# The way back of an FFT convolution: 32-row TensorE tiles, 32x32 transposes on VectorE, and another token order

## The chip, the cores and the metric

The kernel runs on one core of a Trainium2 chip. The metric is the device time of one execution in microseconds (us). The kernel before was run three times; its time is the median of the three. A profile comes from one further execution. Engines are named as in the profile: PE is TensorE's matrix products and PEld its weight loads, DVE is VectorE, ACT is ScalarE, POOL is GpSimd, SP is SyncE, whose queue issues nearly all transfers.

## The reference

One layer of a model: a gated long convolution and an MLP, each behind a layernorm whose scale and shift come from a conditioning vector. There are 2048 tokens and 640 channels, everything in float32.

```python
mod = (silu(c) @ w_mod)                  # six rows of 640: sa, ca, ga, sb, cb, gb
h = layernorm(x) * (1 + ca) + sa         # x is A_q, 2048 x 640
# k_shift: causal convolution of k with 4 taps a channel
kv = k_shift * v
# causal convolution over all 2048 tokens, channel by channel, by FFT of length 4096
y = irfft(rfft(kv, 4096) * rfft(ssm_k, 4096))[:2048] + kv * ssm_D
x = x + ga * (h * y)
h = layernorm(x) * (1 + cb) + sb
out = x + gb * (relu(h @ w1 + b1) ** 2 @ w2 + b2)
```

## The kernel before

**Transform part.** Channels go in five blocks of 128 (index b). The FFT of length 4096 is written as matrix products in two steps each way, with tables `cw` and `gb` on the way there and `gi` and `ca` on the way back. For a block the kernel does this:

- `kv_load`, `kv_k`, `kv_s`, `kv_v`, `kv_m` (four pieces of 512 tokens): load k and v, transpose them with TensorE into PSUM, apply the four taps on VectorE (`kv_s` reads the transposed k, `kt`, from PSUM), multiply by v, and store to the scratch `kv_d`. `load_x` brings that back with time split over the partitions; `load_h` does so for the filter.
- `unit_a` (first step there): 32 products with 64x64 tiles of the array, evicted by ACT into `AX`.
- `front(b, j)`, j = 0 to 7: `spectrum` of the filter (`h`) and of the data (`x`) with `gb`, in two halves of 64 columns; the complex product by VectorE and POOL into `wr` and `wi`.
- `back(b, j)`, j = 0 to 3, one for two fronts: first step back. 16 products with a 64x128 stationary piece of `gi`, in two row halves of 64, into two PSUM tiles `qp` of 512 columns, which two ACT copies scatter into `QT`.
- `unit_t(b, g)`, g = 0 to 7: four 128x128 transposes of `QT` by TensorE into PSUM, then one ACT copy of 512 columns to SBUF.
- `unit_y(b, g)`: second step back. 16 products of 64 moving columns with `ca` as the moving operand; after each second one, 512 columns of y go to the block's tile `UPt`, by ACT for b < 3, by VectorE for b = 3, and for b = 4 as the product with the normalised x that already stands there (the last one in two parts, the second in `y_rest`).
- `prep_a`, `prep_m`, `prep_p`: ACT normalises x into `UT` (for the last block into `UPt`), VectorE scales, POOL shifts. `gate` multiplies by y on VectorE; `finish_near` and `finish_add` add the residual and store to the scratch `x1_d`.

In between stand the products and sums of the conditioning rows (`part_load`, `part_scale`, `part_add`, `mod_row`, `mod_col`) and the statistics of x (`stats1`).

**Order.** Every engine runs its instructions in the order of the program (`keep_order`). For block b there are 10 front slots, FS(b, 0..9), each with a `front` while j < 8 and a `back` at j = 3, 5, 7 and 9; then 18 second-stage slots, GS(b, 0..17) (11 for the last block). The table `tab` puts the rest into slots by hand; the calls of a slot come after its `back` or units, or before them if the slot is in the set `AFTER`. `UNITS` gives for each block the second-stage slots of `unit_a` (of block b + 1), `unit_t` and `unit_y`. Tags name buffers: PSUM has four buffers X, two Y and two T; S4 holds `QT`, S5 `gb`, S6 `gi`, UP0 and UP1 the tiles `UPt`. A tile that reuses a buffer waits until the last reader of the old one is done. Two lines of `tab` that matter:

```python
at(FS(0, 1), (kv_k, 1, 0, "T"), (kv_v, 1, 0), (p_tile, 2))
at(FS(0, 3), (kv_s, 1, 0))
```

and so again at FS(0, 5) and FS(0, 7) for the next piece, and at FS(1, 1) and FS(1, 3) for block 2. `mod_row` and `mod_col` use T as well.

**MLP part.** The hidden layer is computed in 82 steps (`mlp_front`), its squares go to the scratch `h_d` with sums and differences of pairs (a Strassen scheme), and the second product runs over eight blocks of 256 tokens (n) and seven pieces (k): `products`, from k = 0 to 5 the Strassen products into eight accumulators of 320 columns, and for k = 6 the plain products of the last hidden rows into four of them. `evict_first` combines accumulators 0 to 3 into the residual `X2` after k = 5, `evict_rest` adds 4 to 7 at the end of the block. For the last block the order of k is 0, 1, 6, 2, 3, 4, 5, so there both come at the end.

Of the kernel before, what the change touches and what calls it, by code (L numbers as in the profile page):

```python
# [18 lines left out]
P = 128  # L19
# [5 lines left out]
CH = 256  # L25
# [9 lines left out]
def _constants():  # L35
# [16 lines left out]
    gi = np.zeros((2, 64, 2, 64))  # L52
# [10 lines left out]
    gi[0, 1:32, 0], gi[1, 1:32, 0] = 2 * np.cos(ph).T, -2 * np.sin(ph).T  # L63
    gi[0, 0, 0] = 1.0
    gi[1, 0, 0] = (-1.0) ** n1
# [3 lines left out]
    gi[0, 32:, 1], gi[1, 32:, 1] = 2 * np.cos(ph).T, -2 * np.sin(ph).T  # L69

    ca = np.zeros((32, 2, 2, 2, 2, 2, 16, 2))
    t2 = np.arange(16)
    for h in range(2):
        nn = 2 * t2 + h
        th = 2 * np.pi * ((m[:, None] * nn[None, :]) % 64) / 64
        a, b = 2 * np.cos(th) / N, -2 * np.sin(th) / N
        a[0] = 1.0 / N
        b[0] = (-1.0) ** nn / N
        for g in range(2):
            for d in range(2):  # L80
                ca[:, g, d, 0, h, g, :, d] = a
                ca[:, g, d, 1, h, g, :, d] = b
    f = np.float32
    gb = gb.reshape(128, 16, 2, 2, 64).transpose(0, 1, 3, 2, 4)
    gt = gb.transpose(3, 4, 1, 2, 0).copy()
    gt[0, :, 0] = gi.reshape(2, 64, 128).transpose(1, 0, 2)
    return {
        "cw": cw.astype(f),
        "ca": ca.reshape(128, 256).astype(f),
        "gb": gb.reshape(128, 4096).astype(f),  # L90
        "gi": gt.reshape(128, 4096).astype(f),
# [4 lines left out]
def ssm_mlp_kernel(  # L96
# [72 lines left out]
    TS = [WX[i][:, 4 * j : 4 * j + 4] for i in (2, 3) for j in range(2)]  # L169
# [7 lines left out]
    ca = WX[1][:, 8:10].rearrange("p r (h n) -> p r h n", h=2)  # L177
# [186 lines left out]
    gi = sb.tile([P, 16, 2, P], F32, tag="S6", name="gi")  # L364

    def load_gi(i):
        src = gi_d.rearrange("p (g r n) -> p g r n", g=16, r=2)
        sp_dma(gi[:, 4 * i : 4 * i + 4], src[:, 4 * i : 4 * i + 4])
# [89 lines left out]
    def back(b, j):  # L458
        if j == 0:
            QT[b] = sb.tile([P, DG, 32, 4], F32, tag="S4", name=f"q_{b}")  # L460
        end = b == NB - 1 and j == 3
        t = [
            ps.tile(
                [P, 4, P], F32, tag="X" if end else "Y", name=f"qp_{b}_{j}_{a}", bufs=4 if end else 2
            )
            for a in range(2)
        ]
# [1050 lines left out]
```

## Time and profile before

| | |
|---|---|
| runs, us | 677.71, 680.04, 681.62 (median 680.04) |
| profiled execution | 676.89 us, span 675.0 us |
| granted TensorE clock | 0.995 of full speed (mean) |
| transform part | from the start to about 290 us |
| MLP part | from there to the end; last product ends near 668 us |
| transfers | 130.8 MB, 194 GB/s over the span |

The windows are stretches of the span with the busy time of each engine. A row of the chain of waits is start, length, engine, tile and line, and the number of instructions. A row of the groups has line, engine, operation, tiles and shapes, the count, and then busy time and mean length in ns. A row of the timeline is start, length, engine, line, operation, tiles, and in brackets the idle time before it with what ended it. The lengths of PE instructions in the groups include their way through the array, on which the next ones overlap; what a piece takes is better read from the chain.

### The profile page before, as it was taken

How to read it: one execution, taken by the hardware profiler on the slowest of the kernel's cores; microseconds unless marked ns; L12 is line 12 of the kernel's file. 1: busy time of each engine (PE TensorE's matmuls, PEld its weight loads, DVE VectorE, ACT ScalarE, POOL GpSimd, SP SyncE). 2: the span in 40 equal slices, each digit the busy share in tenths (PEclk: the TensorE clock that was granted, in tenths of full speed). 3: DMA queues.
4: the chain of work that ended last, by engine and by line, in shares of the span. 5: the costliest groups of instructions: out<-in, count | busy, mean ns of one | idle time of the engine just before them, and what ended most of it. 6: DMA issues, size and time to landing. Idle time of an engine off the chain costs nothing.

```text
span 675.0 us, 20357 instructions
## 1 busy us (share of the span) xinstructions
PE 635.5 (94%) x8585; PEld 589.0 (87%) x8585; DVE 396.4 (59%) x682; ACT 377.1 (56%) x741; POOL 317.7 (47%) x377
## 2 busy tenths in 40 slices
PE   6788889999989999999999999999989999999995
PEld 5687878789879898889999898898879999999995
DVE  4266566676757689577873175246846445544462
ACT  4535555877875986567785474376763323333230
POOL 1063146459967978846555179328602202221122
PEclk9999899999999999999999999999999999999999
DMA  9698699869555355456644745355375675456641
GB/s 245 202 280 282 161 248 280 239 202 265 151 167 155 110 139 176 118 203 206 223 189 190 248 149 207 145 190 185 104 272 175 230 241 174 154 208 227 219 150 41
DMA packets 108494, 130.80 MB, mean 194 GB/s; under 512 B 21106, under 2 KB 77298, under 8 KB 108404
## 3 DMA queue, kind: packets, MB, share of 16 engines
q1 hardware_dynamic: 106736, 129.30, 61.4%
q8 instruction: 67, 1.10, 0.7%
q10 hardware_dynamic: 1604, 0.21, 0.2%
q14 instruction: 23, 0.19, 0.1%
q0 software_dynamic: 64, 0.01, 0.0%
HBM read 87.03 MB, written 42.47 MB: 192 GB/s over the span
## 4 chain that ended last, share of the span: by engine, by line
PE 80%; ACT 6%; DVE 5%; DMA 4%; issue 3%; POOL 1%; DVEq 0%; POOLq 0%; SPq 0%; ACTq 0%
PE h L811 24%; PE acc L932 21%; PE y L569 6%; PE pa L392 6%; PE qp L473 5%; PE x L407 4%; PE acc L945 3%; PE h L407 3%; PE t L558 2%; PE kt L248 1%; PE xtp L761 1%; PE vt L285 1%; DMA h_d<-wy 1%; DVE wy L154 1%; DMA KV<-in_A_v_dram 1%
## 5 line engine op out<-in xcount | busy, mean ns | idle before, releaser
L160 POOL TENSOR_TENSOR wy<-wy 128x128 f32<-128x128 f32 (+1 forms) x92 | 59.6, 653 | 87.8 <-DVE wy L160 43.1
L157 POOL TENSOR_TENSOR e<-e,e 128x320 f32<-128x320 f32 x16 | 17.5, 1093 | 142.0 <-ACT e L149 142.0
L811 PE MATMUL h<-xt_S,w_S 128*128 128x256 f32 (+2 forms) x425 | 82.4, 308 | 0.0
L860 ACT ACTIVATE wy<-h,b1e 128x256 f32<-128x256 f32 (+1 forms) x77 | 41.9, 544 | 45.3 <-PE h L811 37.0
L392 PE MATMUL pa<-wx,p 64*64 64x64 f32 x2560 | 51.4, 228 | 14.5 <-issue 9.4
L811 PEld LDWEIGHTS h<-xt_S,w_S 128*128 128x128 f32 x425 | 61.8, 189 | 3.7
L392 PEld LDWEIGHTS pa<-wx,p 64*64 64x64 f32 x2560 | 44.9, 140 | 21.7 <-issue 16.8
L149 ACT ACTIVATE a<-pa 128x512 f32<-128x512 f32 x80 | 43.6, 605 | 28.8 <-PE pa L392 28.5
L154 DVE TENSOR_TENSOR wy<-x,wx 128x512 f32<-128x512 f32 x64 | 41.0, 682 | 18.3 <-ACT wx L149 8.5
L811 PE MATMUL h<-xt_XP,w_S 128*128 128x512 f32 (+1 forms) x160 | 50.4, 358 | 0.0
L157 DVE TENSOR_TENSOR wy<-wy 128x128 f32<-128x128 f32 (+1 forms) x36 | 17.9, 498 | 53.5 <-ACT wy L861 41.6
L569 PE MATMUL y<-wy 128*64 128x64 f32 x1280 | 44.9, 226 | 3.7 <-issue 1.9
L569 PEld LDWEIGHTS y<-wy 128*64 128x64 f32 x1280 | 40.5, 139 | 8.2 <-issue 3.8
L149 ACT ACTIVATE h_S<-c_UP 128x896 fp32r<-128x896 f32 (+2 forms) x32 | 25.7, 816 | 39.1 <-PE acc L932 30.6
L407 PE MATMUL x<-a,gb 128*64 128x128 f32 x640 | 41.8, 274 | 3.1 <-DVE wy L154 1.9
L160 DVE TENSOR_TENSOR h_S<-c_UP,h_S 128x896 fp32r<-128x896 f32 (+2 forms) x32 | 30.7, 970 | 23.9 <-ACT h_S L149 23.7
L861 ACT ACTIVATE wy<-wy 128x256 f32<-128x256 f32 (+1 forms) x82 | 40.7, 497 | 2.6
L270 DVE SCALAR_TENSOR_TENSOR KV<-kt,tap,KV 128x511 f32<-128x511 f32 (+2 forms) x48 | 35.9, 747 | 8.0 <-ACT ktail L149 6.3
L407 PEld LDWEIGHTS x<-a,gb 128*64 128x64 f32 x640 | 35.9, 137 | 4.6 <-PE h L407 2.5
L149 ACT ACTIVATE q<-qp 128x512 f32<-128x512 f32 (+1 forms) x40 | 21.2, 583 | 31.8 <-PE qp L473 31.8
L157 POOL TENSOR_TENSOR wm<-wm,wm 128x640 f32<-128x640 f32 x20 | 32.6, 1632 | 8.7 <-ACT wm L350 8.4
L160 POOL TENSOR_TENSOR we<-wy 128x256 f32<-128x256 f32 x20 | 15.8, 791 | 42.4 <-DVE wy L154 42.3
(215 smaller groups left out, 1636.9 us busy)
## 6 DMA issues: line engine op xcount, KB each, us to landing
c_UP<-h_d SPq DMA_DIRECT2D x48, 448.0 KB, 5.4
h_d<-wy SPq DMA_DIRECT2D x24, 448.0 KB, 2.6
h_d<-wy SPq DMA_DIRECT2D x12, 896.0 KB, 4.5
wm<-in_w_mod_dram SPq DMA_DIRECT2D x25, 320.0 KB, 4.6
KV<-in_A_k_dram SPq DMA_DIRECT2D x20, 256.0 KB, 5.1
KV<-in_A_v_dram SPq DMA_DIRECT2D x20, 256.0 KB, 5.2
xp<-in_A_q_dram SPq DMA_DIRECT2D x5, 1024.0 KB, 6.6
x_d<-x SPq DMA_DIRECT2D x8, 640.0 KB, 3.1
```

What stands on the lines that cost most here:

```text
L149: act.activation(o, i, AF.Copy)
L154: eng.tensor_mul(o, a, b)
L157: eng.tensor_add(o, a, b)
L160: eng.tensor_sub(o, a, b)
L270: dve.scalar_tensor_tensor(o, tk[:, : 512 - t], tap[:, b, t : t + 1], o, op0=ALU.mult, op1=ALU.add)
L392: pe.matmul(t[e][64 * r : 64 * r + 64, g].rearrange("p m d -> p (m d)"), pt[b][l, i, 8 * q + g, :], cw[l, r], start=True, stop=True,)
L407: pe.matmul(t[64 * a : 64 * a + 64, s + r], gb[:, g, r, a], AX[b][i][:, 2 * g + a], start=True, stop=True,)
L569: pe.matmul(y[64 * h : 64 * h + 64, 4 * (g % 2) + i].rearrange("p c l d -> p (c l d)"), tss[g][:, i, 64 * r : 64 * r + 64], ca[:, r, h], s ...
L811: pe.matmul(hps[t, f, c0], w, y, start=(b == 0 and i == 0), stop=(b == NB - 1 and i == len(terms) - 1),)
L860: act.activation(z, h.rearrange("p (n s) -> p n s", n=n), AF.Relu, bias=bias)
L861: act.activation(z, z, AF.Square)
L932: pe.matmul(acc[j], h[a][:, c], w[:, y], start=(first and i == 0), stop=(k == NP - 1 and i == 2 and (j < 4 or last)),)
```

## The change

- **Frequency sets.** The outputs of the second step there (`gb`) are ordered so that a tile of 128 rows holds four sets of 32 frequencies, one for each 32-row strip.
- **`back`.** The new `gi` has half the size. Per `back` there are 32 products, each of 32 rows, 64 stationary and 128 moving columns, over four row strips and two column halves, into four PSUM tiles of 256 columns, with the tags Y, Y, T, T. Four copies evict them into `QT`, now channel by 32 frequencies (by ACT; in the last `back` two of them by VectorE).
- **`unit_t`.** Four a block instead of eight. Each is one VectorE instruction that transposes 32x32 blocks of a 128x1024 piece of `QT` into one of two buffers `TT`, in the room that `gi` gave up. TensorE's transposes and their ACT copies are gone.
- **`unit_y`.** Four a block instead of eight: two products each, with `ca` (now 64 columns) stationary and 512 columns moving, into one PSUM tile, one for each column half. The evictions keep their engine, count and size, in another order of elements.
- **Token order.** In SBUF partition and row are now (w, n) and l for token 32n + 16w + l, where they were l·128 + partition. Loads of q and stores of the result go in two transfers of 64 partitions each (`fetch`, `put`).
- **Slots.** `UNITS` has new slots for `unit_t` and `unit_y`; the u tile is asked for at the first `unit_y` instead of the second. `tab` and `AFTER` are as before.
- **The end.** The last token block takes k in the order 0 to 6, `evict_first` does its sums in another order, and the last stores go over SP and ACT by turns, in eight transfers.

```diff
@@ constants: gb's columns reordered; new gi [4, 32, 16, 2, 2, 32] and ca [128, 64] @@
+        c, s = [t.reshape(64, 32, 2).transpose(0, 2, 1).reshape(64, 64) for t in (c, s)]
...
+    s6 = sb.tile([P, 4096], F32, tag="S6", name="gi")
+    gi = s6[:, 0:2048].rearrange("p (g r n) -> p g r n", g=16, r=2)
+    TT = [s6[:, 2048 + 1024 * i : 3072 + 1024 * i].rearrange("p (c n) -> p c n", n=32) for i in range(2)]
...
     def back(b, j):
         if j == 0:
-            QT[b] = sb.tile([P, DG, 32, 4], F32, tag="S4", name=f"q_{b}")
+            QT[b] = sb.tile([P, P, 32], F32, tag="S4", name=f"q_{b}")
         end = b == NB - 1 and j == 3
         t = [
-            ps.tile([P, 4, P], F32, tag="X" if end else "Y", name=f"qp_{b}_{j}_{a}", ...)
-            for a in range(2)
+            ps.tile([P, 2, P], F32, tag="YYTT"[q], name=f"qp_{b}_{j}_{q}", bufs=2)
+            for q in range(4)
         ]
-        for u in range(4):
-            w = ws[b, 2 * j + u // 2]
+        for i in range(2):
+            w = ws[b, 2 * j + i]
             for r in range(2):
-                for a in range(2):
-                    l = slice(64 * a, 64 * a + 64)
-                    pe.matmul(t[a][:, u], gi[l, 4 * j + u, r], w[r][l, u % 2], ...)
+                for q in range(8):
+                    u, q = (q + q // 4) % 2, q % 4
+                    l = slice(32 * q, 32 * q + 32)
+                    pe.matmul(t[q][64 * u : 64 * u + 64, i], gi[l, 4 * j + 2 * i + u, r], w[r][l, u], ...)
...
+        for q in range(4):
+            m = 8 * j + q
+            copy(dve if q % 2 and end else act, QT[b][:, :, m : m + 5 : 4], t[q].rearrange("p i c -> p c i"))
...
+    def tokens(t, l0, n, cols=slice(0, D)):
+        t = t.rearrange("(n w l) d -> w n l d", w=2, l=NL)
+        return [t[w, :, l0 : l0 + n, cols] for w in range(2)]
+
+    def fetch(t, src):
+        for w in range(2):
+            sp_dma(t[64 * w : 64 * w + 64], src[w])
...
-    def unit_t(b, g):
-        t = ps.tile([P, 4, P], F32, tag="T", ...)          # "X" for the last block
-        for i in range(4):
-            pe.transpose(t[:, i], QT[b][:, 4 * g + i].rearrange("p m d -> p (m d)"), ident)
-        copy(act, tss[g], t)
+    def unit_t(b, k):
+        dve.transpose(TT[k % 2], QT[b][:, 32 * k : 32 * k + 32])
+
+    def unit_y(b, k):
+        y = ps.tile([P, 32, NL], F32, tag="Y", name=f"y_{b}_{k}", bufs=2)
+        for w in range(2):
+            pe.matmul(
+                y[64 * w : 64 * w + 64].rearrange("p c l -> p (c l)"),
+                ca,
+                TT[k % 2][:, :, NL * w : NL * w + NL],
+                start=True, stop=True,
+            )
+        x = 16 * (k % 2)
+        uo = UPt[b].rearrange("p l (x e d) -> p x e d l", e=2, d=2)[:, x : x + 16, k // 2]
+        y = y.rearrange("p (x d) l -> p x d l", d=2)
         if b < NB - 1:
+            copy(act if b < 3 else dve, uo, y)
+        elif k < 3:
+            dve.tensor_mul(uo, y, uo)
...
-    seq = [(n, k) for n in range(NC - 1) for k in range(NP + 1)]
-    seq += [(NC - 1, k) for k in (0, 1, NP, *range(2, NP))]
+    seq = [(n, k) for n in range(NC) for k in range(NP + 1)]
...
     UNITS = [
-        ([0, 2, 4, 11, 11, 16, 16], [1, 3, 3, 5, 5, 6, 7, 9], [3, 4, 4, 6, 6, 8, 9, 10]),
-        ([1, 1, 5, 7, 9, 10, 12], [1, 3, 4, 6, 8, 11, 14, 14], [4, 6, 7, 10, 13, 14, 16, 17]),
-        ([1, 3, 5, 7, 8, 11, 14], [1, 3, 5, 7, 9, 11, 12, 15], [4, 6, 8, 9, 12, 14, 16, 17]),
-        ([0, 3, 4, 6, 9, 11, 14], [1, 3, 4, 7, 9, 11, 13, 14], [4, 6, 8, 10, 13, 14, 16, 17]),
-        ([], [1, 1, 2, 2, 5, 5, 6, 7], [4, 4, 5, 6, 6, 8, 8, 10]),
+        ([0, 2, 4, 11, 11, 16, 16], [1, 3, 5, 7], [3, 5, 7, 9]),
+        ([1, 1, 5, 7, 9, 10, 12], [1, 3, 6, 11], [4, 7, 10, 14]),
+        ([1, 3, 5, 7, 8, 11, 14], [1, 5, 9, 12], [4, 8, 12, 16]),
+        ([0, 3, 4, 6, 9, 11, 14], [1, 4, 9, 13], [4, 8, 13, 16]),
+        ([], [0, 1, 2, 4], [1, 2, 4, 6]),
     ]
...
-            if s == sy[1] and not last:
+            if s == sy[0] and not last:
                 u_tile(b)
```

More of the change, by code (lines that the diff above doesn't have):

```diff
@@ L916, in ssm_mlp_kernel, with products @@
     accs = {}
-    def products(n, k, first, last):
-        if first:
+    def products(n, k):
+        if k == 0:
             acc = accs[n] = []
@@ L971, in evict_rest @@
         last = n == NC - 1
-        for j in (3, 0, 1, 2) if last else range(4):
+        for j in range(4):
             s, c = j // 2, (C0, C1)[j % 2]
```

141 lines of the change are left out of this document (56 added, 85 removed).

## The prediction

> **What bounds the kernel now.** First the page's busy times, then the windows of busy time cut at the transform's stages.
>
> ```profile
> span 675.0 us, 20357 instructions
> PE 635.5 (94%) x8585; PEld 589.0 (87%) x8585; DVE 396.4 (59%) x682; ACT 377.1 (56%) x741; POOL 317.7 (47%) x377
> ```
> ```profile
> 39.00:60.00 21.00, 20.56 (x421) 18.71 (x417) 13.53 (x22) 9.30 (x19) 12.91 (x25) 1.00 0.92 272
> 60.00:90.00 30.00, 23.81 (x677) 21.50 (x679) 18.88 (x40) 15.41 (x30) 3.66 (x12) 0.94 0.73 206
> 90.00:117.00 27.00, 26.38 (x466) 24.15 (x463) 18.25 (x32) 15.02 (x27) 17.65 (x26) 1.00 0.94 274
> 117.00:151.00 34.00, 31.63 (x858) 27.72 (x858) 22.16 (x47) 26.87 (x50) 14.76 (x20) 1.00 0.80 225
> 151.00:170.00 19.00, 19.00 (x308) 17.52 (x308) 12.53 (x20) 13.76 (x30) 17.38 (x23) 1.00 1.03 259
> 170.00:202.00 32.00, 27.89 (x837) 24.68 (x835) 20.65 (x33) 27.13 (x57) 24.51 (x26) 1.00 0.58 159
> 202.00:222.00 20.00, 20.00 (x360) 19.24 (x358) 15.64 (x26) 10.94 (x20) 15.71 (x20) 1.00 0.53 143
> 222.00:249.00 27.00, 26.17 (x866) 23.75 (x864) 19.92 (x22) 26.02 (x58) 24.44 (x18) 1.00 0.51 130
> 249.00:273.00 24.00, 22.25 (x376) 20.68 (x373) 20.04 (x27) 15.10 (x33) 17.80 (x22) 1.00 0.50 145
> 273.00:299.00 26.00, 24.36 (x371) 21.54 (x369) 16.89 (x38) 13.76 (x33) 15.41 (x16) 1.00 0.56 178
> ```
>
> After window and length the columns are PE, PEld, DVE, ACT, POOL, granted clock, DMA share and GB/s. Rows alternate: a front stage (spectra, products, `back`) of one channel block, then its second stage (`unit_a`, `unit_t`, `unit_y`). TensorE carries 242 of these 260 us and paces nearly every row; but in the second stages of blocks 2 and 3 ACT and POOL are close behind (26.02 and 24.44 of 27), and DMA fills three of the first five rows. So shorter TensorE work pays only down to the next engine. The rest of the span is the MLP, which the change touches only at its very end.
>
> The chain of waits gives what a TensorE piece takes when nothing else delays it:
>
> ```profile
> 94.37 1.02 PE h L407 x16
> ...
> 98.01 1.99 PE qp L473 x32
> ...
> 113.02 1.09 PE pa L392 x64
> ...
> 122.07 1.08 PE y L569 x32
> 123.15 0.59 PE t L558 x4
> ...
> 286.23 3.43 PE gr L1093 x12
> ```
>
> Each float32 product is two instructions: a `back` issues 16 products and shows 32. The `gr` row has the whole array to itself: 3.43/12 = 286 ns for 320 columns, 0.89 ns a column. By that a 128-column instruction alone is 114 ns; `qp` takes 1.99/32 = 62 ns, so its two 64-row tiles run 1.8 at a time. For `pa`, 57 ns alone, it is 1.09/64 = 17 ns: its four 64x64 tiles run 3.4 at a time, 0.84 of the ideal.
>
> **The change, TensorE.** `unit_t` loses its transposes: 8 x 0.59 = 4.7 us a block. `unit_y` goes from 8 x 1.08 to four sets of two products of 512 columns, four instructions. Alone they would be 4 x 458 ns = 1.83 us; two column halves at 0.84 of ideal give 1.09. I take 1.09, because `h` (also two 64-column halves, 1.02/16 = 64 ns against 114) overlaps that way: 8.6 − 4.4 = 4.3 us saved. `back` issues 64 instructions of 32 rows, 64 columns and 128 moving columns. No row shows eight tiles. At eight and `pa`'s efficiency: 114/(8 x 0.84) = 17 ns, 1.09 us; at four 34 ns, 2.17 us; at two, as `qp` now, 62 ns, 3.97 us. I take 1.09: `pa` is the nearest row, because it too divides both rows and columns, and 17 ns an instruction is a rate that it already sustains. Saved: 4 x 0.90 = 3.6 us. In all 12.6 us a block, 63 over five.
>
> The Trainium skill speaks against this: "TensorE: Matmul & The Clock Gate", Part 1 (Wait — 56ns, not 53.3ns?) says that matmul starts are never closer than about 25 ns. By that, as an estimate, a `back` would be 64 x 25 = 1.6 us and the saving 1.6 us a block, some 4 us less in the sum. The `pa` row's 17 ns disagrees, so the sum does not use it; it stands among the rivals.
>
> **The change, other engines.**
>
> ```profile
> L149 ACT ACTIVATE wy<-t 128x512 f32<-128x512 f32 x40 | 23.4, 607 | 8.2 <-PE t L558 8.1
> ...
> L149 ACT ACTIVATE q<-qp 128x512 f32<-128x512 f32 x38 | 20.6, 594 | 30.9 <-PE qp L473 30.9
> ...
> L747 ACT ACTIVATE xt_S<-xtp,cbs 128x256 fp32r<-128x256 f32 x20 | 8.6, 468 | 1.1 <-PE xtp L761 1.0
> ```
> ```profile
> L154 DVE TENSOR_TENSOR up<-up,KV 128x512 f32<-128x512 f32 x16 | 19.2, 1215 | 0.0
> ...
> L740 DVE TENSOR_SCALAR mtmp<-x,rs,nm 128x640 f32<-128x640 f32 x7 | 4.5, 639 | 0.3
> ```
>
> ACT drops eight copies of 607 ns a block and evicts a `back` with four 256-element copies (468) for two of 594: −4.9 + 2.7 = −2.2 us. The y copies keep size and count; their writes scatter, which I put at nothing: ACT has the room just made, and without that cover some 0.1 us each. VectorE gains four transposes of 1024 elements a block. No row shows one. Lower bound, the 640-element row: 1.0 ns an element, 1.02 us; upper, the slowest two-input row: 1215/512 = 2.4 ns, 2.4 us. I take 1.15, since a transpose reads one input as the 640 row does: +4.6 us a block. The Trainium skill's "Vector Engine (DVE) Microarchitecture Reference", section 3.8, has a transpose sustain one element per cycle per lane; that leaves the chosen end as it is.
>
> **What room that leaves.** Per window, length less the next engine. 60:90: VectorE 18.9 + 4.6 = 23.5, room 6.5. 90:117: DMA 0.94 x 27 = 25.4, room 1.6. 117:151: DMA 27.2, room 6.8. 151:170: DMA full, none. 170:202: VectorE 25.3, room 6.7. 202:222: TensorE itself 16.4, room 3.6. 222:249: VectorE 24.5, room 2.5. 249:273: VectorE 20.0, room 4. Without 90:117 (and 39:60), taken below, 30.1 us. The engines keep a written order and will wait for one another, so not all is won; nothing in the trace fixes the share. I take two thirds, −20, and keep none and all for the range.
>
> **What takes some back.**
>
> ```profile
> 41.41 2.06 PE L473 MATMUL qp<-we,gi 64*128 64x128 f32 x32
> ...
> 42.90 2.30 DVE L270 SCALAR_TENSOR_TENSOR KV<-kt,tap,KV 128x511 f32<-128x511 f32 x3
> ...
> 50.63 2.06 PE L473 MATMUL qp<-we,gi 64*128 64x128 f32 x32
> ...
> 53.09 2.31 DVE L270 SCALAR_TENSOR_TENSOR KV<-kt,tap,KV 128x511 f32<-128x511 f32 x3
> ```
>
> `back` now needs both T buffers of PSUM. In block 0's front stage `kv_k` holds one, and the `kv_s` that frees it comes after that `back`. So the first waits until 42.90 + 2.30 = 45.2 and, less 0.9 of its products, ends near 46.1 instead of 43.5 (+2.6); the third until 55.4, near 56.3 instead of 52.7 (+3.6). Everything in TensorE's queue waits behind them: the next spectra, and with them VectorE and POOL. The other two backs give 0.9 each: +4.4, of which I let window 60:90, where TensorE idles 6 us, absorb 1.4: +3. Block 1 has one such case: +2.6, less 0.6: +2.
>
> In the last block VectorE becomes a chain. Before:
>
> ```profile
> 273.52 0.76 DVE L151 COPY q<-qp 128x256 f32<-128x256 f32 x2 [2.34 <-PE qp L473]
> 274.20 1.41 DVE L160 TENSOR_TENSOR w_S<-w1s,w_S 128x640 fp32r<-128x640 f32 x1
> 275.70 1.59 DVE L154 TENSOR_TENSOR up<-up,g1row 128x512 f32<-128x512 f32 x1
> ...
> 277.38 1.48 POOL L157 TENSOR_TENSOR up<-up,s1row 128x512 f32<-128x512 f32 x1 [0.63 <-DVE xt_S L160]
> 278.15 0.98 DVE L157 TENSOR_TENSOR x<-xp,up 128x256 f32<-128x256 f32 x1
> ...
> 279.06 0.68 DVE L584 TENSOR_TENSOR up<-y,up 128x512 f32<-128x512 f32 x1
> ...
> 286.16 3.50 PE L1093 MATMUL gr<-w_gate 128*128 128x320 f32 x12
> ```
>
> Now, from the end of `qp` at 273.5: copies 0.8, w1 split 1.4, first transpose 1.15, the u product 1.1–1.6; its POOL add (1.5) lets the first y product start near 280.2 rather than 279.06. Then the second transpose 1.15, y 1.1, product 0.7, third transpose 1.15, the two residual adds (the second 0.98) with statistics, some 1.9, product 0.7, fourth transpose 1.15, y 1.1: near 289.7 `gr` starts, 3.5 later. I take +3 (transposes of 2.4 would make it +8).
>
> **End, queues, copies.**
>
> ```profile
> 46.42 0.45 SPq L142 DMA_DIRECT2D KV<-in_A_v_dram  x1
> ```
> ```profile
> 652.87 2.92 PE acc L945 x20
> ```
> ```profile
> 665.52 0.44 ACT L149 ACTIVATE e<-acc 128x320 f32<-128x320 f32 x1 [8.75 <-PE acc L932]
> ...
> 667.08 1.06 PE L932 MATMUL acc<-w_S,h_S 128*128 128x320 f32 x6
> ...
> 670.24 0.86 POOL L157 TENSOR_TENSOR wy<-wy,e 128x320 f32<-128x320 f32 x1
> 671.13 0.89 DVE L157 TENSOR_TENSOR wy<-acc,wy 128x320 f32<-128x320 f32 x2 [0.86 <-POOL wy L157]
> ```
>
> The last token block's plain products move to the end, the 2.92 us of the `acc` L945 row; the sums before them can start that much earlier under them, so the tail from 665.5 is hidden by 2.9: −3. SP loses two `gi` issues and gains about 13 half loads and 11 half stores; most lie where SP waits for buffers, and if that cover goes they are 0.45 us each (first row), about 5 us in block 1's crowded queue. `gi`'s lost megabyte helps window 39:60 alone, where the T wait decides. The second block's y copies now ask for their u buffer two slots earlier, while POOL still reads block 0's: ACT waits there, inside the third that I do not count.
>
> **Sum.** −20 + 3 + 2 + 3 − 3 = −15. The profiled execution took 676.9 us (span 675.0), 3.1 below the median 680.0: 662 against itself, 665 against the median, which I forecast.
>
> **Rivals.** (1) The engines pack well, all room is won and the T waits vanish in slack: −36 + 3 − 3, 644; for it, TensorE's load, against it, fixed orders. Chance 0.13. (2) Eight tiles overlap less than `pa`'s four: midway between 17 and 34 ns an instruction a `back` is 1.6 and half of its gain goes, 669; at four tiles 2.17, each +0.2 instead of −0.9: rows 202:222 and 249:273 lose their 5 and gain 1.5, other rows 3: 674. The 25 ns of the Trainium skill's page "TensorE: Matmul & The Clock Gate", Part 1, would be the first of these. Chance 0.14. (3) The added waits and VectorE's turns eat the gain (share a quarter instead of two thirds): 678. Chance 0.09. (4) Slower: only two 32-row tiles run at once, as the two 64-row tiles of `qp` do. Then `back` is 3.97, +2.0 each, twenty of them in rows that TensorE fills: −15 + 5 + 40 = +30, 710. It decides from about 2.5 us a `back`, 39 ns an instruction. For it: no row shows more than four tiles; against: `pa`. Chance 0.09. (5) Slower: a transpose costs above 2.4 us, which lengthens 222:249 to 30 and the last block by 8, around 685. Chance 0.05.
>
> **How the numbers follow.** The likeliest case keeps 0.50, with a range of its own of 654 to 672 (half to all of the room, and T waits as worked out or gone). The range 647 to 681 leaves out most of (4), half of (5) and part of (1). A measurement of this kernel tells 0.5%, 3.4 us: faster by more than that holds the likeliest case, (1), most of (2), a third of (3): 0.77; within 0.5% 0.09; slower 0.14.
>
> **What would show it.** `qp` as 64 instructions in about 1.1 us (right), 2.2 or 4 (wrong, by 2 or 4); `t` gone from TensorE; y in about 1.1 us a set; VectorE transposes near 1.15 us; TensorE waits on `kv_s` in the `qp` of block 0; `gr` starting later after the last `qp` by about 3 us; a shorter last store tail by 3. The prediction is wrong if windows of the second stages keep their length although TensorE idles.

## The result and the profile after

The changed kernel took 713.8 us (median of 4, 706.6 to 716.3) beside 678.9 for the kernel before: 1.0502 times its time, interval 1.0447 to 1.0556. The forecast was 665, the range ended at 681. The profiled execution took 715.5 us, of which 713.7 are the span. One run of e1, three of e13 and one of e18 below fell into a slower state; the figures of these kernels are those of their other runs.

The page's first part, after, then the first VectorE instruction of the MLP on the tile `xt_S` in both kernels (after, before; the times behind the durations are first and last start):

```profile
span 713.7 us, 18931 instructions
PE 617.4 (86%) x7865; PEld 543.8 (76%) x7865; DVE 416.7 (58%) x702; ACT 375.9 (53%) x739; POOL 316.2 (44%) x377
```
```profile
L759 DVE SCALAR_TENSOR_TENSOR xt_S<-xtp,cbs,xt_S x10: 432/476/484, 332.6 to 346.5; 128x256 fp32r<-128x256 f32 x10
```
```profile
L751 DVE SCALAR_TENSOR_TENSOR xt_S<-xtp,cbs,xt_S x10: 430/474/484, 290.4 to 304.8; 128x256 fp32r<-128x256 f32 x10
```

TensorE has 18 us less work and the span 38.7 us more. All of it lies ahead of the MLP, which begins 42.2 us later; from there to the end the kernel is 3.5 us shorter (713.7 − 332.6 against 675.0 − 290.4). The windows of the transform, cut again at the stages (columns as in the prediction: PE, PEld, DVE, ACT, POOL, clock, DMA share, GB/s):

```profile
36.00:70.00 34.00, 24.02 (x548) 20.61 (x544) 15.78 (x26) 11.69 (x25) 14.37 (x27) 0.80 0.54 139
70.00:99.00 29.00, 19.64 (x434) 12.66 (x434) 23.50 (x45) 14.86 (x26) 3.87 (x12) 0.82 0.89 216
99.00:132.00 33.00, 27.14 (x588) 23.05 (x584) 18.06 (x32) 15.94 (x32) 16.91 (x26) 0.90 0.94 229
132.00:168.00 36.00, 26.16 (x568) 18.33 (x568) 24.44 (x48) 24.62 (x43) 14.89 (x20) 0.91 0.84 216
...
196.00:229.00 33.00, 20.36 (x565) 14.58 (x566) 22.70 (x34) 25.38 (x52) 21.34 (x24) 0.83 0.52 126
...
252.00:278.00 26.00, 18.83 (x524) 14.38 (x510) 21.32 (x23) 20.52 (x47) 21.68 (x15) 0.75 0.54 125
278.00:307.00 29.00, 23.43 (x514) 20.42 (x510) 20.49 (x28) 18.18 (x40) 19.47 (x23) 0.91 0.52 125
307.00:332.00 25.00, 13.91 (x39) 5.42 (x36) 15.77 (x27) 4.82 (x11) 10.07 (x12) 0.54 0.41 124
sum 296.00, PE 218.38 PEld 169.00 DVE 194.76 ACT 167.59 POOL 160.84; mean PE 21.84 PEld 16.90 DVE 19.48 ACT 16.76 POOL 16.08
```

Read three columns. TensorE no longer fills its windows (218 of 296 us, before 242 of 260). No other engine has taken its place: the next one stands at 195, and only the DMA engines come near full, with shares of 0.89 and 0.94 in the rows from 70 and 99. And the granted clock, 0.94 or 1.00 in every row before, is now 0.54 to 0.93. A kernel that no engine fills is one in which the engines wait for one another, or for transfers.

The second stages of blocks 0 to 3 (the rows from 70, 132, 196 and 252) take 29, 36, 33 and 26 us, 124 in all. The prediction's rows for them have 30, 34, 32 and 27, 123 in all. TensorE is busy in them for 85.0 us, where it was for 109.5. This is the sign that the prediction named for being wrong: second stages that keep their length although TensorE idles.

What TensorE waited for, after (us in total, times, longest):

```profile
PE y L579 <- DVE gi L574: 21.8, 9, 3.9
PE qp L486 <- DVE KV L282: 13.2, 4, 4.5
PE pa L406 <- issue: 10.9, 5, 4.6
PE pa L406 <- ACT a L162: 7.6, 1, 7.6
PE qp L486 <- issue: 4.9, 3, 2.6
```

These are, in order, the VectorE transposes, the T buffers, TensorE with nothing to wait for that the profile shows ("issue"), the u tile of block 2, and "issue" again. The timeline of TensorE (start, us, engine, line; in brackets the idle time before it and what ended it; one row is of ACT, with the wait of block 2's y copy for its u tile) shows that a wait costs more than its own length:

```profile
44.70 1.99 PE L486 MATMUL qp<-we,gi 32*64 32x128 f32 x58 [3.50 <-DVE KV L282]
...
51.08 1.21 PE L486 MATMUL qp<-wy,gi 32*64 32x128 f32 x64
...
61.22 1.99 PE L486 MATMUL qp<-we,gi 32*64 32x128 f32 x58 [4.49 <-DVE KV L282]
...
64.19 1.99 PE L406 MATMUL pa<-wx,p 64*64 64x64 f32 x64
```
```profile
209.00 1.06 ACT L162 ACTIVATE up<-y 128x512 f32<-128x512 f32 x1 [5.54 <-POOL xp L170]
```
```profile
212.71 1.98 PE L406 MATMUL pa<-wx,p 64*64 64x64 f32 x60 [7.56 <-ACT a L162]
...
220.09 1.08 PE L579 MATMUL y<-gi,wy 128*64 128x512 f32 x4
```
```profile
319.80 1.97 PE L579 MATMUL y<-gi,wy 128*64 128x512 f32 x4 [2.35 <-DVE gi L574]
324.12 1.97 PE L579 MATMUL y<-gi,wy 128*64 128x512 f32 x4 [2.35 <-DVE gi L574]
326.02 5.46 PE L1098 MATMUL gr<-w_gate 128*128 128x320 f32 x12
```

Undisturbed, 64 `qp` instructions take 1.2 us, as forecast. Fifty-eight of such a group behind a wait of 3.5 us take 1.99, `pa` 1.99 instead of 1.09, y 1.97 instead of 1.08, `gr` 5.46 instead of 3.43. The Trainium skill's "TensorE: Matmul & The Clock Gate", section "Why this matters for your kernels", says that TensorE gaps of more than about 3 us bring the clock back to half; the trace agrees (waits of 3.50, 4.49 and 7.56 us, durations up to 1.8 times as long). The trace adds that in the last block, with a clock of 0.54 over the row from 307, y and `gr` were slow behind waits of only 2.35 us as well.

Summed by groups over the transform (after from 36 to 332 us, then before from 35 to 290; busy, mean ns):

```profile
L406 PE MATMUL pa<-wx,p 64*64 64x64 f32 x2048 | 46.3, 250 | 19.3 <-issue 10.0 <-ACT a L162 7.6 <-DMA p<-kv_d 1.3
...
L579 PE MATMUL y<-gi,wy 128*64 128x512 f32 x80 | 30.0, 825 | 21.8 <-DVE gi L574 21.8
L486 PE MATMUL qp<-wy,gi 32*64 32x128 f32 x640 | 18.4, 308 | 4.5 <-issue 2.6 <-DVE KV L282 1.1 <-ACT q L162 0.8
L486 PE MATMUL qp<-we,gi 32*64 32x128 f32 x640 | 16.2, 314 | 14.4 <-DVE KV L282 12.1 <-issue 2.3
```
```profile
L569 PE MATMUL y<-wy 128*64 128x64 f32 x1280 | 44.9, 226 | 3.7 <-issue 1.9 <-ACT wy L149 1.8
...
L392 PE MATMUL pa<-wx,p 64*64 64x64 f32 x2048 | 40.4, 225 | 9.6 <-issue 8.6 <-DVE KV L292 0.6 <-POOL p L157 0.3
```

`pa` is the same work in both kernels and took 5.9 us more; y took 30.0 where 20 sets of 1.08 are 21.6; the 20 `back`s 34.6 where 20 of 1.2 are 24. That is 25 us more in three groups alone, on top of the idle time to their right. Not all of it need be the clock's: the last `qp` group of the kernel, with waits of less than 1 us ahead of it, spread over 2.78 us.

### The profile page after: what moved, and what is told of

It reads as the page before. It is cut to its first block, busy times and chain, and to the rows that moved or that the text cites. A ratio compares the mean times of both kernels' runs of the same rounds, so it can differ in the third digit from the quotient of the medians.

```text
span 713.7 us, 18931 instructions
## 1 busy us (share of the span) xinstructions
PE 617.4 (86%) x7865; PEld 543.8 (76%) x7865; DVE 416.7 (58%) x702; ACT 375.9 (53%) x739; POOL 316.2 (44%) x377
## 4 chain that ended last, share of the span: by engine, by line
PE 70%; DVE 10%; DMA 5%; ACT 5%; issue 5%; POOL 3%; SPq 0%; POOLq 0%; DVEq 0%; ACTq 0%
PE h L819 26%; PE acc L939 20%; PE x L421 4%; PE qp L486 4%; PE h L421 4%; PE acc L952 3%; PE pa L406 3%; DVE KV L282 3%; PE y L579 2%; POOL wm L170 2%; DVE wy L167 1%; ACT q L162 1%; PE xtp L769 1%; DVE gi L574 1%; DMA kv_d<-KV 1%
## 5 line engine op out<-in xcount | busy, mean ns | idle before, releaser
L406 PEld LDWEIGHTS pa<-wx,p 64*64 64x64 f32 x2560 | 51.0, 159 | 37.1 <-issue 19.0
L406 PE MATMUL pa<-wx,p 64*64 64x64 f32 x2560 | 56.9, 247 | 24.7 <-issue 10.9
L162 ACT ACTIVATE q<-qp 128x256 f32<-128x256 f32 x78 | 37.9, 638 | 41.9 <-PE qp L486 41.9
L421 PE MATMUL x<-a,gb 128*64 128x128 f32 x640 | 46.2, 291 | 5.5 <-ACT wx L162 4.2
L579 PE MATMUL y<-gi,wy 128*64 128x512 f32 x80 | 30.0, 825 | 21.8 <-DVE gi L574 21.8
L421 PEld LDWEIGHTS x<-a,gb 128*64 128x64 f32 x640 | 40.1, 148 | 7.0 <-ACT wx L162 4.4
L421 PE MATMUL h<-a,gb 128*64 128x128 f32 x512 | 37.9, 295 | 3.3 <-ACT wx L162 3.3
L173 POOL TENSOR_TENSOR we<-wy 128x256 f32<-128x256 f32 x20 | 15.8, 790 | 52.0 <-DVE wy L167 45.9
L421 PEld LDWEIGHTS h<-a,gb 128*64 128x64 f32 x512 | 31.9, 149 | 7.2 <-ACT wx L162 3.6
```

What stands on the lines that cost most here:

```text
L162: act.activation(o, i, AF.Copy)
L173: eng.tensor_sub(o, a, b)
L406: pe.matmul(t[e][64 * r : 64 * r + 64, g].rearrange("p m d -> p (m d)"), pt[b][l, i, 8 * q + g, :], cw[l, r], start=True, stop=True,)
L421: pe.matmul(t[64 * a : 64 * a + 64, s + r], gb[:, g, r, a], AX[b][i][:, 2 * g + a], start=True, stop=True,)
L579: pe.matmul(y[64 * w : 64 * w + 64].rearrange("p c l -> p (c l)"), ca, TT[k % 2][:, :, NL * w : NL * w + NL], start=True, stop=True,)
```

## The experiments

**The pauses, one at a time.** e1 and e12 free the T buffers in two ways, e2 asks for block 2's u tile, with its first y set, two slots later, e3 starts the last block's transposes earlier.

```
e1   kv_s of (1,0), (1,1), (2,2): FS(0,3) -> FS(0,2), FS(0,7) -> FS(0,6), FS(1,3) -> FS(1,2)
e12  at(FS(0, 1), (kv_k, 1, 0, "T") -> "X"; the same for (1,1), (2,2), (2,3)
e2   UNITS[2], y slots: [4, 8, 12, 16] -> [6, 8, 12, 16]
e3   UNITS[4], transposes: [0, 1, 2, 4] -> [0, 0, 1, 2]
```

> The changed kernel with kv_s of three pieces one front slot earlier, so that it stands ahead of the back that needs its T buffer. Theory A (TensorE waits for buffers and for VectorE's turns, and each pause of some us also halves the granted clock for the pieces behind it): the waits of qp on kv_s, 3.50 + 4.49 + 4.09 us, fall to under 1 each, and the pieces behind them (qp 1.99, x 1.91, pa 1.99) go back to 1.1: 12 to 16 us less, near 700. Rival B (slow scattered writes of ACT and VectorE set the pace): the waits are hidden by ACT's backlog, 0 to 4 us less. Rival C (the second stages have slack that takes it all): 0 to 4 us less, with window 60 to 100 longer by as much.

> The changed kernel with one edit: the four k tiles that stood in the T buffers of the front stages (blocks 1 and 2) stand in X buffers instead, so no qp tile shares a buffer with them. Theory (a TensorE pause costs itself and the half clock of the work behind it): the qp waits for DVE KV (13.2 us in 4) go, with the 0.85 us by which each qp group after them was longer; 695 to 702 us. Rival (the waits were only their own length, and X, which holds the outputs of the front and of pa, becomes the new wait): 708 to 716 us, with the waits of pa, x or h for an X buffer in their place.

> The changed kernel with the first unit_y of the third block two slots later (6 for 4), and with it the u tile. Theory A: ACT's wait of 5.54 us for POOL's reading of the old u tile and TensorE's 7.56 us behind it go; 5 to 8 us less, near 707. Rival C (POOL's order sets this stage anyway, as its finish_add comes at the same time): 0 to 2 us less.

> The changed kernel with the last block's transposes ahead of the y product before them on VectorE (slots 0, 0, 1, 2 for 0, 1, 2, 4). Theory A: y of one piece runs under the transpose and product of another; the last block's second stage, 307 to 326 us in the trace, loses 3 x 1.97 us of y waits less what remains, 4 to 6 us less, near 709. Rival D (the granted clock, 0.54 there, is what makes it long): y stays at 1.97 and only some 2 us go.

Measured (in brackets the ratio to the kernel before and its 95% interval): e1 702.9 (1.0335 [1.0281, 1.0389]), e12 700.6 (1.0293 [1.0239, 1.0346]), e2 703.8 (1.0367 [1.0308, 1.0426]), e3 707.3 (1.0427 [1.0375, 1.048]); against the changed kernel 10.9, 13.3, 10.0 and 6.5 us less. By the ratios, which take out differences between groups of runs, it is 11, 14, 9 and 5 us, each known to about 5 us. So the gains of e1, e12 and e2 are clear, and that of e3 is at the edge: its interval overlaps that of the change.

In e12 `qp` waits for `KV` no longer (13.2 us in the change), in e2 the 7.6 us wait for ACT is gone, and e1 leaves 8.1 us of the waits for `KV`. In e12 and e2 the gain is about as long as the waits that went, in e1 it is 6 us longer; within 5 us these runs can't tell what the slow instructions behind a wait add. In e3 TensorE's waits for the transposes only fall from 21.8 to 19.8 us over the kernel, but the trace shows the gain where it was sought: from the start of the last `qp` group to `gr` 21.7 us became 15.7. Each of the three waits is a real cause.

**The clock by itself.** e8 puts eight products of the identity ahead of each y set in the last block, so that TensorE isn't idle while it waits.

```
+        if b == NB - 1:
+            z = ps.tile([P, P], F32, tag="X", name=f"z_{k}", bufs=4)
+            for _ in range(8):
+                pe.matmul(z, ident, ident, start=True, stop=True)
```

> The changed kernel with eight idle products (128x128 by 128, result not used) ahead of each y set of the last block, where TensorE waits 2.4 to 3.9 us for VectorE. Rival D (clock): the granted clock of that stage goes from 0.54 to near 1, y from 1.97 to 1.1 us and the following gr from 5.46 to about 3.5; 4 to 6 us less, near 709, though TensorE does more work. Theory without the clock: y stays at 1.97 since its two halves run one after the other, and the time stays or grows by up to 4.

Measured: 707.8, 1.0412 [1.0351, 1.0474], 6 us less than the changed kernel. The chain in the last block:

```profile
318.32 1.09 PE y L583 x4
...
325.95 1.08 PE y L583 x4
327.03 3.43 PE gr L1102 x12
```

With TensorE kept busy, y takes 1.08 and `gr` 3.43 again: the long durations come from the pause, not from the instructions. In the traces the stage from the start of the last `qp` group to the first `xt_S` takes 24.2 us in place of 28.3, so some 4 us of the slow clock's price are seen here. The total can't confirm it: the intervals of this run and of the change overlap.

**Scattered copies.** e4 stores q by frequency so that ACT writes it densely (the transposes then read 4-byte elements 512 bytes apart), and orders y's copies by tokens, in pairs of neighbours.

```
-copy(act, QT[b][:, :, m : m + 5 : 4], t[q].rearrange("p i c -> p c i"))
+copy(act, QT[b][:, m : m + 5 : 4], t[q])
-dve.transpose(TT[k % 2], QT[b][:, 32 * k : 32 * k + 32])
+dve.transpose(TT[k % 2], QT[b][:, :, 32 * k : 32 * k + 32].rearrange("p m c -> p c m"))
-uo = UPt[b].rearrange("p l (x e d) -> p x e d l", e=2, d=2)[:, x : x + 16, k // 2]
+uo = UPt[b].rearrange("p l (x e d) -> p l x e d", e=2, d=2)[:, :, x : x + 16, k // 2]
```

> The changed kernel with other element orders in the copies, same counts: qp goes in runs of 128 elements to a Q tile stored frequency by channel (the VectorE transpose then reads with a stride), y is written in pairs of neighbours. Rival B: qp copies fall from 638 ns to about 470 (78 of them, 13 us of ACT), y copies from 1074 to about 640 (12, 5 us) and VectorE's y work from 1.04 to 0.69 (8, 3 us); 10 to 20 us less, 695 to 704. Theory A: ACT is not what TensorE waits for at most places; 3 to 7 us less, from the last block (8 of these in its chain) and the T and Y buffers that come free earlier. If the transpose reads with a stride at twice its time (1.23 to 2.4 us, 20 of them), the gain is lost or turned.

Measured: 713.0, 1.0478 [1.0404, 1.0552], no change. Groups of the transform, after and then e4:

```profile
L162 ACT ACTIVATE q<-qp 128x256 f32<-128x256 f32 x78 | 37.9, 638 | 41.9 <-PE qp L486 41.9
...
L162 ACT ACTIVATE up<-y 128x512 f32<-128x512 f32 x12 | 12.9, 1074 | 13.6 <-POOL xp L170 5.5 <-PE y L579 4.8 <-issue 3.3
```
```profile
L574 DVE STREAM_TRANSPOSE gi<-q 128x1024 f32<-128x1024 f32 x20 | 24.6, 1230 | 9.5 <-ACT q L162 9.5
```
```profile
L162 ACT ACTIVATE q<-qp 128x256 f32<-128x256 f32 x78 | 23.7, 390 | 43.0 <-PE qp L486 42.9
L162 ACT ACTIVATE up<-y 128x512 f32<-128x512 f32 x12 | 7.7, 643 | 15.1 <-POOL xp L170 6.4 <-PE y L579 5.4 <-issue 3.3
```
```profile
L574 DVE STREAM_TRANSPOSE gi<-q 128x1024 f32<-128x1024 f32 x20 | 38.8, 1939 | 6.5 <-ACT q L162 6.5
```

The scatter is dear (638 against 390 ns, 1074 against 643), but dense q only hands the bill to the engine that reads it: 14 us less on ACT, 14 more on VectorE. The y copies save ACT another 5. The order of q has to be paid once; e4 doesn't show what each part would be worth alone.

**VectorE's transposes.** e11 makes one a block in place of four.

```
-        dve.transpose(TT[k % 2], QT[b][:, 32 * k : 32 * k + 32])
+        if k == 0:
+            dve.transpose(TT[0], QT[b][:, 0:32])
```

> The changed kernel with one transpose a block in place of four; all four y sets of a block read the first one's output, so this leaves out three quarters of the VectorE transposes and the waits of y for them, and its y values are those of the first set. Theory (y's waits for VectorE, 21.8 us in 9, and the half clock after them, 8 us on y and 2 on gr, are the largest single part of the loss): 685 to 697 us. Rival (the waits for VectorE lie beside other lateness, of ScalarE's q copies and of the loads): 705 to 714 us.

Measured: 707.5, 1.041 [1.0348, 1.0472]: 6.3 us less than the change, in the rival's range, though TensorE's waits for transposes fell by 12.8 us, from 21.8 to 9.0. So in the changed kernel these waits are worth about half of their length, as far as a difference with an uncertainty of 5 us can tell; the rest lies beside other lateness.

**Together.** e6 holds e1, e2, e3 and e4. e9 holds e12, e2, e3 and the y copies of e4, with q scattered as in the change. e10 adds eight identity products ahead of every y set, into the y tile itself.

> The four edits before this together: kv_s ahead of back, the third block's u tile later, the last block's transposes ahead, dense copies. Theory A with B: the gains add, as they lie in different stages: 25 to 40 us less than the changed kernel, 675 to 690, about the time of the kernel before. If the forecast's room was there, under 670. Rival E (instruction supply: TensorE stops for 1.5 to 4.6 us without a wait, 15.8 us in the changed kernel against 11.5 before) leaves it above 690 with these stops unchanged.

> The changed kernel with four edits: k tiles in X buffers, u tile of block 2 back at slot 6, the last block's transposes one slot earlier, and the y copies in a dense order (the q copies stay scattered, the transposes read dense rows). Theory that the loss is the sum of these pauses: the single gains of about 10, 10 and 6.5 us add up, 684 to 692 us, below the 695.0 of the version that also made the q copies dense, since VectorE is spared 14 us of longer transposes. Rival (the gains overlap, and what is left is instruction supply and VectorE's turns): 693 to 702 us.

> The kernel of e9 with eight idle products of the identity (275 ns each, 2.2 us) written into each y tile ahead of its four real ones, in all blocks. Theory that the clock after a pause is a cost of its own: y goes from 1.97 to 1.08 us and what follows it runs at full clock, but the 20 sets also pay 2.2 us each wherever they did not wait (some 13 of 20, 29 us at most, hidden where VectorE or ScalarE sets the pace): between 3 us faster and 15 us slower than e9; the granted clock of the transform rises either way. Rival (the clock is no cost, only a reading of idleness): slower than e9 by 25 us or more and no shorter y.

Measured: e6 695.0 (1.0209 [1.0154, 1.0264]), e9 688.8 (1.0119 [1.0058, 1.018]), e10 694.0 (1.0198 [1.0136, 1.026]). e6 missed its range and came out as its rival E had it, above 690, with 16.2 us of "issue" waits left (15.8 in the change). In e9 the three waits add up, nearly: 13.3 + 10.0 + 6.5 = 29.8 apart, 25.0 together. Groups of e9 and then of e10:

```profile
L406 PE MATMUL pa<-wx,p 64*64 64x64 f32 x2048 | 45.4, 246 | 15.6 <-issue 12.0 <-POOL p L170 1.4 <-DMA p<-kv_d 0.9
...
L579 PE MATMUL y<-gi,wy 128*64 128x512 f32 x80 | 27.9, 787 | 21.0 <-DVE gi L574 19.1 <-ACT up L162 1.9
```
```profile
L579 PE MATMUL y<-ident 128*128 128x128 f32 x320 | 43.6, 293 | 0.7 <-ACT q L162 0.7
...
L581 PE MATMUL y<-gi,wy 128*64 128x512 f32 x80 | 21.6, 618 | 3.7 <-DVE gi L574 3.7
```

In e10 TensorE does 43.6 us of idle work and the kernel takes 5.2 us more (the intervals of the two overlap): the rest lies in waits or comes back as shorter instructions (y 27.9 to 21.6). The clock is a cost, but idle products are no way to save it here. e9 is still 8 us above before, though it has the new tail.

**The new tail alone**, on the kernel before: the last token block's products in plain order, its evictions and four stores as in the change.

> The kernel before with only the change's end: order of k 0 to 6 in the last token block, the new order of evict_first, last stores by turns over SP and ACT (in four transfers, old token order). The forecast's step: 3 us less than the kernel before, about 676 against 679. Rival: no difference beyond 1 us.

Measured: 675.3, 0.9933 [0.9901, 0.9965], 4.7 us less. So e9's transform is some 13 us slower than that of before.

**What else: late instructions, or the loads.** e13 and e14 leave the k and v loads of blocks 1 to 4 out, of e9 and of before. e15 is e9 with whole q and xp loads in the old order; e17 is before with the halved loads of the change.

```
e13, e14  kv_load:   +        if b:
                     +            return
e15       fetch:     -        for w in range(2):
                     -            sp_dma(t[64 * w : 64 * w + 64], src[w])
                     +        sp_dma(t, src)          # src: q[...].rearrange("(l p) d -> p l d", p=P)
e17       load_xp, q_load of before: the two halves of the change in place of one sp_dma
```

> The kernel of e9 without the k and v loads of blocks 1 to 4 (8.4 MB of some 48 in the transform; their products are made of block 0's rows, so the output leaves those inputs out). Theory that the pauses in which TensorE waits for nothing visible are instructions that come late because the DMA engines are full of data: pa's 12.0 us of such waits fall below 5, none longer than 2.5 us, and the time falls by 8 to 15 us against e9 (674 to 681). Rival (they belong to the instruction stream, whatever the loads do): the waits stay at 10 us or more and the time within 4 us of e9.

> The kernel before without the same k and v loads (blocks 1 to 4), as the control. Theory: it has 18 us of such waits in its chain, in pieces of 2.1 us at most that pa already partly hides, so it gains less than e9 does from the same cut: 2 to 6 us (674 to 678). Rival (a lighter load helps every kernel alike, so it explains none of the difference between them): as much as e9 gains.

> The kernel of e9 with the q and xp loads in one transfer of 128 partitions each and the token order of before, where e9 has two of 64 partitions (this leaves out the new token order, so q rows stand in other places; bytes and products are the same). Theory (two transfers of half the partitions are slower: 640 KB landed in 9.7 us where 1280 KB took 7.7, and the DMA share per GB/s rose): DMA share of the early windows falls, the waits for loads (pa for kv_d, xt for q) with it; 680 to 685 us. Rival (transfers are hidden anyway, the pauses decide): 687 to 691 us.

> The kernel before with only its q and xp loads changed to the new form, two transfers of 64 partitions each in the new token order (the rest keeps the old order, so the sum of x and y mixes tokens). Theory (the half transfers cost by themselves): 4 to 9 us slower than before (684 to 689). Rival (hidden): within 2 us of before.

Measured: e13 680.8 (1.0024 [0.9971, 1.0077]), 6.5 us below e9 by the ratios; e14 677.7 (0.9951 [0.9917, 0.9986]), 3 us below before by the ratio; e15 678.6 (0.9985 [0.9947, 1.0022]), 10.2 below e9 (9 by the ratios); e17 692.6 (1.0189 [1.0122, 1.0257]), 13.9 above before, more than its theory had. So the halved loads hold it. Whether lighter traffic helps e9 more than it helps before isn't clear of the noise (6.5 and 3 us). In e13 TensorE's "issue" waits for `pa` fell from 12.0 to 4.5 us, as its theory had it, but those for `qp` rose from 0.9 to 7.9, with one of 4.1.

The DMA queue of the data from 36 to 290 us (packets, MB, share of 16 engines), the large q loads (size, median us to landing), and TensorE's waits for "issue": before, and then before with halves (e17).

```profile
q1 hardware_dynamic: 59939, 49.70, 69.6%
...
q<-in_A_q_dram SPq DMA_DIRECT2D x2, 1280.0 KB, 7.7
```
```profile
PE pa L392 <- issue: 9.4, 10, 2.1
...
PE y L569 <- issue: 1.9, 1, 1.9
```
```profile
q1 hardware_dynamic: 55523, 46.49, 73.8%
...
q<-in_A_q_dram SPq DMA_DIRECT2D x4, 640.0 KB, 10.5
```
```profile
PE pa L392 <- issue: 15.4, 8, 4.9
PE y L571 <- issue: 6.9, 3, 4.6
```

In e17 half a load lands later than a whole one did, and the queue takes 13% more of the engines' time for each byte (73.8/46.49 against 69.6/49.70). The second holds in every run: this quotient, for the same 254 us, is 1.40 to 1.43 with whole loads (before, e14, e15, e19, e21) and 1.59 to 1.62 with halves (the change, e9, e13, e17). Landing times overlap more: 7.6 to 10.0 us for 1280 KB whole, 6.5 to 10.5 for 640 KB halves. TensorE's "issue" waits double, 11.3 to 22.3 us, and the longest goes from 2.1 to 4.9 us, with no change in TensorE's program. That they are instructions that come late through the same DMA engines (the page lists an instruction queue) fits e17 and e15 (`pa` 6.3 us, longest 2.7). It doesn't fit e14: with fewer loads all of TensorE's "issue" waits stay at 12.1 us (11.5 before), with one of 4.9. No run shows the instruction's own transfer, so the cause of these waits stays open.

**Halves or addresses.** On the kernel before: e18 halves the loads and keeps the order; e19 keeps whole loads and lets partition p read 16 tokens in a row.

```
e18  for w in range(2): sp_dma(t[64 * w : 64 * w + 64], src[64 * w : 64 * w + 64])
e19  sp_dma(t, q.rearrange("(p l) d -> p l d", p=P)[:, l0 : l0 + n])
```

> The kernel before with each q and xp load cut into two transfers of 64 partitions, token order unchanged. Theory H (transfers of half the partitions are slow, whatever they read): 8 to 14 us slower than before, as with halves and the new order together (692.6). Theory O (the new order's addresses are slow: each partition reads one long run, 1280 or 2560 bytes times the rows, and neighbours lie 16 or 32 rows apart): within 3 us of before.

> The kernel before with its q and xp loads as single transfers of 128 partitions, but partition p reading the 16 tokens from 16 p on (long runs, neighbours 16 rows apart; the rest keeps the old order, so the sum of x and y mixes tokens). Theory O: 8 to 14 us slower than before. Theory H: within 3 us of before.

Measured: e18 695.7, 1.0265 [1.0179, 1.0351], even more than theory H had; e19 679.4, 1.0018 [0.9982, 1.0055]. It is the halving. The Trainium skill gives a reason that these runs fit, though none of them shows the ports: "SBUF — State Buffer", section "Door 1: The DMA port swizzle", says that partitions 0 to 63 reach only half of the memory's DMA ports, and "DMA: Bandwidth & Descriptors", section "Rules for kernel authors", says to use one transfer of 128 partitions, since two halves follow one another.

**The change without halves.** e21 is e9 with partition p holding tokens 16 p to 16 p + 15, so loads and stores are whole; y's table is padded with zeros, and the two products of a set add up in one tile.

```
-                y[64 * w : 64 * w + 64].rearrange("p c l -> p (c l)"),
-                ca,
+                y.rearrange("p c l -> p (c l)"),
+                ca[:, w],
...
-                start=True,
-                stop=True,
+                start=(w == 0),
+                stop=(w == 1),
```

> The kernel of e9 with the two halves of y interleaved: partition p holds the 16 tokens from 16 p on, so every load and store of tokens is one transfer of 128 partitions. For that y's table is padded with zeros to 128 columns for each half, and the two products of a set add into the whole tile one after the other (some 2.2 us a set in place of 1.08). Nothing of the computation is left out. Theory (halved transfers cost 10 us here, TensorE has slack): 676 to 684 us, level with the version that kept whole loads in the old order, plus at most 5 us for the longer y and less the tail's whole stores. Rival (TensorE's 22 us more work lies on the path): 688 to 700 us.

Measured: 676.8, 0.9982 [0.9948, 1.0016], level with before within the noise. Its groups, waits and the start of the MLP:

```profile
L576 PE MATMUL y<-gi,wy 128*128 128x512 f32 x80 | 46.2, 710 | 16.4 <-DVE gi L571 12.2 <-ACT up L162 2.3 <-DVE KV L304 1.8
...
L406 PE MATMUL pa<-wx,p 64*64 64x64 f32 x2048 | 39.7, 225 | 8.5 <-issue 6.2 <-POOL p L170 1.4 <-DVE KV L304 0.8
```
```profile
L756 DVE SCALAR_TENSOR_TENSOR xt_S<-xtp,cbs,xt_S x10: 431/474/484, 291.6 to 306.0; 128x256 fp32r<-128x256 f32 x10
```

y is as long on TensorE as it was before the change (46.2 and 44.9 us), and still 12.0 us are gained on e9 (9 by the ratios): whole loads and stores are worth more than 18 us of TensorE's work. `pa` is back at 225 ns. The MLP starts at 291.6, against 332.6 in the change and 290.4 before. So the way back to the time before is 713.8 − 25.0 (the three waits, and the y copies, not measured alone) − 12.0 (halves) = 676.8. These are differences along one row of kernels, which must add up; they say what each step was worth, and not why the forecast gain is missing.

## Why the prediction was wrong

The step that failed is the room: −20 us, two thirds of what lay between TensorE and the next busiest engine in each window. None of it was won. e15, with the T waits, the u tile and the loads mended and y short, is level with before and has the tail's 4.7 us, so its transform is no faster than that of before; by the ratios of e15 and e7 it is some 3 us slower, about as much as the noise. Busy time from 36 to 290 us, e15 and then before:

```profile
sum 254.00, PE 203.13 PEld 156.74 DVE 196.08 ACT 161.26 POOL 161.80; mean PE 22.57 PEld 17.42 DVE 21.79 ACT 17.92 POOL 17.98
```
```profile
sum 254.00, PE 236.07 PEld 213.83 DVE 174.46 ACT 168.89 POOL 162.65; mean PE 26.23 PEld 23.76 DVE 19.38 ACT 18.77 POOL 18.07
```

TensorE is busy for 33 us less (the prediction counted 63 less work), VectorE for 22 more. TensorE now idles for 51 of the 254 us and VectorE for 58, and the time is the same. So the busy time of a window's busiest engine was a lower bound that this kernel doesn't reach. TensorE's largest waits in e15 are those of y for VectorE's transposes (16.4 us). That the order written by hand decides, with VectorE, ACT and TensorE handing one tile round, fits these waits but wasn't tested by another order. For e15 the prediction's terms are −20 and −3; measured is 0. What would have to change to win the room stays open.

In rough numbers, −15 was forecast and +35 measured. Of these 50 us the room is 20, the T waits are 8 more than their +5, the u tile is 10, the half loads are 9 to 12 and the last block about 3, each known to some 5 us.

Point by point:

- **TensorE's work: right.** `qp` 1.21 us for 64 instructions, 19 ns each (forecast 1.09 and 17, so eight tiles do overlap), y 1.08 (1.09), `t` gone. Rivals (2) and (4) are out.
- **Transposes: right in price** (1.23 us, forecast 1.15), so rival (5) is out; and less on the path than their waits look (e11: 6 us for three quarters of them).
- **T waits: right in place, too small.** They came where they were put; +3 and +2 were the terms, 13.3 is the measured value (e12).
- **u tile: mis-sized.** It was put inside the third of the room that wasn't counted. It held ACT for 5.54 us and TensorE for 7.56, and cost 10.0 (e2).
- **Last block: mis-sized.** +3 was the term. VectorE's chain is as described, but with TensorE waits of 2.35 to 3.94 us ahead of y sets of 1.97. `gr` started 18.9 us after the end of the last `qp` in place of 12.7, 6.2 later where 3.5 was forecast, and took 5.46. e3 got 6.5 back.
- **Copies: wrong in price.** 638 ns against 468 taken, and y's 1074 against 636 before, 0.44 us more where some 0.1 was taken. What they cost in time isn't shown, since e4 moves the scatter of q to VectorE.
- **Half loads: the second step that failed.** They were counted as 0.45 us of SP issue each, hidden. The transfers themselves cost 13.9 us and more on the kernel before (e17, e18) and 9 to 12 in the mended change (e15, e21).
- **Tail: right.** −3 forecast, −4.7 measured (e7).
- **Rivals (1) and (4).** The −36 of (1) is more than the prediction's rows give: 30.1, and 33.4 with 90:117 and 39:60. That (4)'s 710 lies near the measured time is chance, as its mechanism didn't occur.

What no rival had is the clock: in the traces the longer pauses also stretch what follows them. The clock column stood at 0.94 or 1.00 in the windows quoted, and the prediction left it there. Its price could be told apart in one place only, some 4 us of the last block (e8); in e12 and e2 the gains match the waits alone within the noise, and e10 shows no net gain from mending it. So it adds to the loss and does not explain it. Rival (3), added waits and turns that eat the gain, had the right direction, but it stopped at a gain of about 2 us.

## What to carry to other kernels

Room between two engines in a window is not time to be won: follow the tile from engine to engine. Price a pause of TensorE that nothing else covers at its whole length (e12, e2); one that lies beside other lateness is worth less (e11, about half). Expect slower instructions behind a long pause, too. A new layout is costed at its loads and stores too: ask how many partitions each transfer now writes, because here two of 64 were slower than one of 128, and the whole kernel became longer by it (e17, e18). When a layout forces halves, look for one that interleaves; e21 paid for it with 18 us of TensorE's work and came out ahead of e9.

## What the runs showed of the hardware

- TensorE's mean clock was 0.54 in a 25 us window with four waits of 2.4 to 3.9 us; y took 1.97 us there, 1.08 where TensorE had not waited (220.09 us), and 1.08 again when idle products filled the waits (e8).
- Eight float32 tiles of 32 rows by 64 columns ran at 19 ns an instruction (64 in 1.21 us).
- ACT wrote 256 elements in 390 ns in runs of 128 elements and in 638 in 4-byte pieces; 512 elements in 643 ns in pairs of neighbours and in 1074 in 4-byte pieces (e4 and the change).
- A 32x32 transpose of 128x1024 float32 took 1.23 us from dense rows and 1.94 from elements 512 bytes apart.
- Loads of 64 partitions in pairs: 640 KB landed in 10.5 us (e17), where one of 128 partitions brought 1280 KB in 7.7 (before). Halving these loads took 13% more of the DMA engines' time for each byte, and the kernel became 13.9 us longer.
